# Windowed attention and a two-layer MLP in split fp32: half of the lower weights made on GpSimd, one slice's split queued behind the first activations, four weight loads at another place

## The chip, the cores and the metric

The kernel runs on one core of a Trainium2 chip. A core has TensorE (matmul), VectorE, ScalarE and GpSimd, each with its own queue of instructions, and SyncE, whose queue issues nearly all DMAs here. In the profile they are called PE, DVE, ACT, POOL and SP. The metric is device time in microseconds (us), the median over runs.

## The reference

Batch 8, 8 heads, 512 local and 32 global positions, head size 64; then an MLP of 4352 tokens (8 x 544), width 512, hidden width 2048.

```python
s_g   = scale * q_g @ [k_g, k_l].T               # global queries see all positions
out_g = softmax(s_g) @ [v_g, v_l]
s_ll  = where(|i - j| <= 32, scale * q_l @ k_l.T, -1e9)
s_l   = [scale * q_l @ k_g.T, s_ll]              # local queries see a window and the global keys
out_l = softmax(s_l) @ [v_g, v_l]
x = concat(out_g, out_l), heads side by side     # (4352, 512)
h = x @ w_in                                     # w_in (512, 2048), delivered as float64
out = (h * sigmoid(h)) @ w_out                   # w_out (2048, 512), delivered as float64
```

## The kernel before

**Split numbers.** The MLP's operands are kept as two fp32r numbers, an upper part (the rounded value) and a lower part (the rest); a product is three matmuls: upper by upper, lower by upper, upper by lower. `xh`/`xl` are the parts of x, `gh`/`gl` those of the activations, `w_hi`/`w_lo` those of the weights.

**Weights.** The hidden width is cut into 16 slices f of 128. A slice has two halves of 128x512: half 0 belongs to `w_in` (read by `first_layer`), half 1 to `w_out` (read by `second_layer`). A half goes through three steps. `fetch_weights(f, half)` issues its load, 512 KB of 64-bit words, on SyncE's queue. `join_weights` makes fp32 of it (L221 on ScalarE, L223 and L224 on VectorE). `split_weights(f)` makes both halves' parts: for each half a cast on ScalarE (L233) and a subtraction w - w_hi on VectorE (L234). `raw_w12`, say, is half 0 of slice 6, `raw_w13` half 1 of slice 6. All this is done once, while block 0 runs; the parts then stay in SBUF.

**The MLP.** Tokens come in 12 blocks n of 3 tiles (the last two of 2). For each block, f runs over the 16 slices: `first_layer(n, f)` does 12 matmuls (L625) into `h`, then tanh (L632, ScalarE), one VectorE operation (L633), the cast `gh` (L635, ScalarE) and the rest `gl` (L636, VectorE). `second_layer(n, f-1)` of the slice before follows on TensorE with 9 matmuls (L652), then `first_layer(n, f+1)`, and so on.

**Attention.** It comes in steps k (one chunk of 128 queries, one pair of heads), laid between the MLP's matmuls by `fill`. A step loads q and k (`st_load`, tile `raw`), computes scores (L381 on TensorE), adds the mask (L388, VectorE, from PSUM), takes exp (L392, ScalarE), scales by the reciprocal of the sum (L394, L395 on VectorE; L399, L401 on ScalarE), and is transposed. From step 12 on the transposition goes over DMA: two copies on GpSimd (L413, `halves`), a DMA out (`away`), and a transposing DMA back (`pt`). `st_out` (L464) makes x from it, with `xh` (L471) and `xl` (L472). The global queries have steps of their own (`gs`, `pg`: L266, L269, L292 to L297).

**Order.** TensorE's instructions run in the order in which the program is written. For the other engines a scheduler orders them by its own estimate, save that those wrapped in `hold` keep the program's order among themselves. Each engine works through its queue in order. The steps of attention and the first loads of weights are put on a line of due times (`put(when, ...)`) and sorted. The table `FIRSTW` says which halves are fetched at which step k; `PASSW` says which at slice f of block 0; the remaining ones are fetched five slices ahead (`FETCH`). Slices 0 and 1 are split ahead of block 0. In block 0, at slice f >= 1, `split_weights(f + 1)` and the joins two slices ahead come before `first_layer(0, f)`.

Of the kernel before, what the change touches and what calls it, by code (L numbers as in the profile page):

```python
# [9 lines left out]
F32 = mybir.dt.float32  # L10
# [6 lines left out]
ALU = mybir.AluOpType  # L17
# [12 lines left out]
NCC, NF = DM // P, DFF // P  # L30
# [21 lines left out]
FETCH, LOOK = 5, 3  # L52
PLACES = ("ws15", "ws14", "ws13", "klo", "ws14", "ws15", "klo", "qk")
FIRSTW = {4: ((0, 0), (0, 1)), 5: ((1, 0), (1, 1)), 6: ((2, 0),), 7: ((2, 1),), 8: ((3, 0), (3, 1)),
          9: ((4, 0), (4, 1)), 10: ((5, 0), (5, 1), (7, 0)), 11: ((8, 1), (6, 1))}
PASSW = {0: ((7, 1), (9, 1)), 1: ((10, 1),)}
JOINS, SPLITS = (9.0, 9.6, 10.2, 10.8, 11.4, 12.0), (12.1, 12.7)

FIRST = dict(load=(-1.2, -1.1, -1.0, 0.1), vload=(1.22, 1.23, 2.22, 2.23), turn=(3.2, 4.0, 4.9, 5.8), out=(4.3, 5.2, 6.1, 7.0),
# [9 lines left out]
HEADS0, HEADS = (11, 1), (7, 2)  # L69
TURN1, TURN, TURND = (0.65, 1.5), (0.4, 1.5), (0.4, 0.45)  # L70
FULL = 0.98
END = 0.5

@with_exitstack
def attention_moe_kernel(ctx: ExitStack, tc: tile.TileContext, qk0_in, qk_in, v_in, gqk, wts, out):
    nc = tc.nc
# [27 lines left out]
    hold = tc.keep_in_program_order  # L104
# [83 lines left out]
    w_32, w_hi, w_lo, w_raw, w_next = [], [], [], {}, [0]  # L188
# [18 lines left out]
    def join_weights():  # L207
        i = w_next[0]
        w_next[0] += 1
        f = i // 2  # L210
        if f + 1 == NF:
            w_32.append(work.tile([P, SKV], F32, tag="klo", bufs=BUFS["qk"], name=f"w{i}")[:, :DM])
        elif i % 2 == 0:
            w = const.tile([P, 2 * DM], F32, tag=f"ws{f + 1}", name=f"w{f}")
            w_32.extend((w[:, :DM], w[:, DM:]))
        for raw, c0, n in w_raw[i]:
            join_words(w_32[i][:, c0 : c0 + n], raw)
# [9 lines left out]
    def split_weights(f):  # L227
        w_hi.append(const.tile([P, 2 * DM], F32R, tag=f"wh{f}", name=f"w_hi{f}"))
        w_lo.append(const.tile([P, 2 * DM], F32R, tag=f"ws{f}", name=f"w_lo{f}"))
        for c0 in range(0, 2 * DM, DM):  # L230
            sl = slice(c0, c0 + DM)
            hi, lo, w = w_hi[f][:, sl], w_lo[f][:, sl], w_32[2 * f + c0 // DM]
            hold(nc.scalar.copy(out=hi, in_=w))  # L233
            hold(nc.vector.tensor_tensor(out=lo, in0=w, in1=hi.bitcast(F32), op=ALU.subtract))  # L234


    state = {}
# [279 lines left out]
    at = 0.0  # L517

    def put(when, fn, *a):
        stream.append((when, fn, a))  # L520
# [3 lines left out]
    for k, (t, b, c, pr) in enumerate(steps):  # L524
# [12 lines left out]
        if k == AHEAD:  # L537
# [7 lines left out]
            at = FIRST["then"]  # L545
# [6 lines left out]
                put(at + (TURN1 if b < 2 else TURN if b < GD else TURND)[hh], g_turn, b, hh)  # L552
        for f, half in FIRSTW.get(k, ()):
            put(at + 0.01, fetch_weights, f, half)
        ats.append(at)
        put(min(at + due["load"], ats[k - 3] + BEFORE) if k >= ND + 3 else at + due["load"], st_load, *a)
        put(at + due["split"], st_split, *a)
# [9 lines left out]
        if k < SINGLE or pr == NPR - 1:  # L567
            n = 1 if k < SINGLE else NPR
# [27 lines left out]
    ends, t = [], 0  # L596
    for s in SIZES:
        t += s
        ends.append(marks[t - 1] + END)

# [3 lines left out]
    def fill(part):  # L604
# [4 lines left out]
        if n + 1 < len(SIZES):  # L609
            advance(ends[n] + (ends[n + 1] - ends[n]) * min(1.0, now[1] / total / FULL))  # L610

# [6 lines left out]
    def first_layer(n, f):  # L618
        nt = SIZES[n] * P
        xh, xl = xblk[n]  # L620
        h = ps_h.tile([P, 512], F32, tag="h", name=f"h{n}_{f}")
        i = 0
        for wt, x in ((w_hi[f], xh), (w_hi[f], xl), (w_lo[f], xh)):
            for c in range(NCC):
                nc.tensor.matmul(h[:, :nt], wt[:, c * P : (c + 1) * P], x[:, c, :nt], start=(i == 0),  # L625
                                 stop=(i == 3 * NCC - 1))
                i += 1
        t = two.tile([P, 3 * P], F32, tag="t", bufs=1, name=f"t{n}_{f}")
        gh = two.tile([P, 3 * P], F32R, tag="gh", name=f"gh{n}_{f}")
        gl = two.tile([P, 3 * P], F32R, tag="gl", name=f"gl{n}_{f}")  # L630

        nc.scalar.activation(t[:, :nt], h[:, :nt], AF.Tanh, scale=0.5)  # L632
        nc.vector.scalar_tensor_tensor(out=t[:, :nt], in0=t[:, :nt], scalar=1.0, in1=h[:, :nt], op0=ALU.add,  # L633
                                       op1=ALU.mult)
        nc.scalar.copy(out=gh[:, :nt], in_=t[:, :nt])  # L635
        nc.vector.tensor_tensor(out=gl[:, :nt], in0=t[:, :nt], in1=gh[:, :nt].bitcast(F32), op=ALU.subtract)  # L636
        return gh, gl

    def second_layer(n, f, gh, gl):
# [37 lines left out]
    for n in range(len(SIZES)):  # L677
        for f in range(NF):
            if n == 0:
                split_weights(f + 1) if 0 < f < NF - 1 else None  # L680
                while w_next[0] < 2 * min(NF, f + LOOK):
                    join_weights()
                for g, half in PASSW.get(f, ()):
                    fetch_weights(g, half)
                for g, half in ((f + FETCH, 0), (f + FETCH - (f + FETCH > SCRATCH), 1)):
                    if g < NF and 2 * g + half not in w_raw:
                        fetch_weights(g, half)
            elif f == 0:
                advance(ends[n])
                now[:] = n, 0  # L690
            g = first_layer(n, f)
            fill(SIZES[n])
            if pend is not None:
                second_layer(*pend)
            pend = (n, f, *g)
# [70 lines left out]
```

## Time and profile before

| | |
|---|---|
| median of 3 runs | 965.1 us (964.55 to 967.78) |
| the profiled execution | 964.87 us, span of its profile 962.7 us |
| TensorE busy | 940.6 us (98%) |
| VectorE busy | 629.9 us (65%) |
| ScalarE busy | 574.2 us (60%) |
| GpSimd busy | 217.1 us (23%) |

Times in the profile are counted from the start of the span. Block 0 begins at 47 us and ends at about 142 us; the weights are joined and split from 31 to 133 us. A row of the timeline gives start, duration, engine, line, operation, output <- inputs and their shapes; what stands in brackets is the engine's idle time before it and what ended that.

### The profile page before, as it was taken

What the parts mean: (1) busy time and instruction counts of PE and PEld (TensorE: products, weight loads), DVE (VectorE), ACT (ScalarE), POOL (GpSimd) and SP (SyncE); (2) the same over time, 40 slices, a digit from 0 to 9 for tenths busy, and PEclk for the clock granted to TensorE, in tenths of its full rate; (3) what the DMA queues carried; (4) which work ended last, traced back from release to release, by engine and by line L of the source; (5) the groups of instructions that cost most, each with busy time, mean ns of one, the idle gap of its engine ahead of it and who ended that gap; (6) DMA issues with size and microseconds to landing.
All of it is one profiled execution on the core that took longest, in us unless ns stands there. A gap on an engine that the chain in (4) does not pass through costs nothing.

```text
span 962.7 us, 17396 instructions
## 1 busy us (share of the span) xinstructions
PE 940.6 (98%) x5734; PEld 840.9 (87%) x5734; DVE 629.9 (65%) x1893; ACT 574.2 (60%) x1475; POOL 217.1 (23%) x433
## 2 busy tenths in 40 slices
PE   8789999999999999999999999999999999999998
PEld 6578888999998999989999899998999899989897
DVE  5889977766876677655677677766677656453322
ACT  7888876656656566544665656665566555443322
POOL 2112322122332223122133222222223221120000
PEclk9999999999999999999999999999999999999999
DMA  8989966577668675743856776686775864532000
GB/s 301 350 226 262 266 170 187 158 171 213 172 157 211 168 192 147 193 116 86 223 158 167 201 172 188 159 206 170 170 216 148 201 147 130 144 93 66 1 22 23
DMA packets 201306, 162.57 MB, mean 169 GB/s; under 512 B 139392, under 2 KB 159360, under 8 KB 201216
## 3 DMA queue, kind: packets, MB, share of 16 engines
q1 hardware_dynamic: 196800, 153.52, 59.9%
q10 hardware_dynamic: 4416, 7.93, 2.3%
q8 instruction: 46, 0.75, 0.3%
q14 instruction: 44, 0.36, 0.1%
HBM read 86.44 MB, written 41.94 MB: 133 GB/s over the span
## 4 chain that ended last, share of the span: by engine, by line
PE 83%; DVE 4%; ACT 2%; issue 1%; DMA 0%; DVEq 0%; ACTq 0%
PE h L625 36%; PE out L652 35%; PE o L464 6%; PE s L383 2%; PE s L384 2%; DVE w_lo L234 1%; DVE w L224 1%; PE gs L275 1%; PE gs L276 1%; DVE probs L388 1%; DVE klo L366 0%; DMA raw<-in_qk_dram 0%; DVE raw_w L223 0%; ACT probs L392 0%; DVE t L633 0%
## 5 line engine op out<-in xcount | busy, mean ns | idle before, releaser
L413 POOL COPY halves<-probs 128x512 uint16<-128x512 uint16 x232 | 154.9, 694 | 436.2 <-ACT probs L399 234.6
L632 ACT ACTIVATE t<-h 128x384 f32<-128x384 f32 (+1 forms) x192 | 90.6, 472 | 172.5 <-PE h L625 156.9
L633 DVE SCALAR_TENSOR_TENSOR t<-t,h 128x384 f32<-128x384 f32 (+1 forms) x192 | 101.6, 529 | 105.9 <-ACT t L632 104.8
L652 PE MATMUL out<-w_hi,gh 128*128 128x512 f32 x544 | 164.2, 400 | 2.5 <-ACT gh L635 2.5
L625 PE MATMUL h<-xh,w_hi 128*128 128x384 f32 (+1 forms) x768 | 160.0, 330 | 1.9 <-ACT w_hi L233 1.9
L652 PE MATMUL out<-w_lo,gh 128*128 128x512 f32 x544 | 161.2, 394 | 0.0
L652 PE MATMUL out<-w_hi,gl 128*128 128x512 f32 x544 | 161.0, 394 | 0.0
L625 PE MATMUL h<-xl,w_hi 128*128 128x384 f32 (+1 forms) x768 | 158.2, 327 | 0.0
L625 PE MATMUL h<-xh,w_lo 128*128 128x384 f32 (+1 forms) x768 | 158.2, 327 | 0.0
L392 ACT ACTIVATE probs<-probs,st 128x224 f32<-128x224 f32 x244 | 115.8, 475 | 62.8 <-DVE st L388 62.1
L625 PEld LDWEIGHTS h<-xh,w_hi 128*128 128x128 f32 x768 | 132.9, 188 | 17.4 <-ACT w_hi L233 3.6
L636 DVE TENSOR_TENSOR gl<-t,gh 128x384 fp32r<-128x384 f32 (+1 forms) x192 | 110.3, 575 | 43.1 <-ACT gh L635 40.9
L388 DVE CUSTOM_DVE_ANT_0 probs<-s,mask 128x224 f32<-128x224 f32 x244 | 85.8, 387 | 80.2 <-PE s L384 70.8
L625 PEld LDWEIGHTS h<-xl,w_hi 128*128 128x128 f32 x768 | 132.8, 188 | 0.0
L625 PEld LDWEIGHTS h<-xh,w_lo 128*128 128x128 f32 x768 | 131.3, 188 | 0.5 <-DVE w_lo L234 0.3
L635 ACT CAST gh<-t 128x384 fp32r<-128x384 f32 (+1 forms) x192 | 94.5, 492 | 57.8 <-DVE t L633 57.6
L652 PEld LDWEIGHTS out<-w_hi,gl 128*128 128x128 f32 x544 | 100.3, 188 | 22.2 <-DVE gl L636 0.5
L652 PEld LDWEIGHTS out<-w_lo,gh 128*128 128x128 f32 x544 | 100.5, 188 | 21.7 <-issue 0.6
L652 PEld LDWEIGHTS out<-w_hi,gh 128*128 128x128 f32 x544 | 93.8, 189 | 13.3 <-ACT gh L635 4.7
L365 ACT CAST qk<-raw 128x704 fp32r<-128x704 f32 x100 | 77.5, 775 | 7.7 <-DMA raw<-in_qk_dram 5.2
L366 DVE TENSOR_TENSOR klo<-raw,qk 128x448 fp32r<-128x448 f32 x100 | 66.2, 662 | 18.2 <-ACT qk L365 16.7
L399 ACT ACTIVATE probs<-probs,st 128x224 f32<-128x224 f32 x118 | 56.7, 481 | 30.2 <-DVE st L395 28.7
(96 smaller groups left out, 1065.7 us busy)
## 6 DMA issues: line engine op xcount, KB each, us to landing
raw<-in_qk_dram SPq DMA_DIRECT2D x100, 352.0 KB, 3.2
away<-halves SPq DMA_DIRECT2D x116, 256.0 KB, 2.3
vraw<-in_v_dram SPq DMA_DIRECT2D x30, 512.0 KB, 5.1
raw_w<-in_wts_dram SPq DMA_DIRECT2D x29, 512.0 KB, 6.4
raw_g<-in_gqk_dram SPq DMA_DIRECT2D x32, 304.0 KB, 3.1
out_dram<-o ACTq DMA_DIRECT2D x29, 256.0 KB, 3.3
raw<-in_qk_dram SPq DMA_DIRECT2D x28, 240.0 KB, 4.6
gaway<-pg SPq DMA_DIRECT2D x10, 256.0 KB, 2.1
```

Of the source, the lines that this page charges most:

```text
L365: nc.scalar.copy(out=qk, in_=raw)
L366: nc.vector.tensor_tensor(out=klo[:, :KW], in0=raw[:, QW:], in1=qk[:, QW:].bitcast(F32), op=ALU.subtract)
L388: nc.vector.tensor_tensor_reduce(out=p[:, u, :W], in0=ss[u], in1=mask_of[c], scale=-SCALE, scalar=3.0e38, op0=ALU.add, op1=ALU.min, accum_ ...
L392: nc.scalar.activation(p[:, u, :W], p[:, u, :W], AF.Exp, bias=st[:, u : u + 1], scale=-1.0, accum_out=st[:, 2 + u : 3 + u])
L413: nc.gpsimd.tensor_copy(out=halves[:, :, u], in_=p[:, 2 * P * u : 2 * P * (u + 1)].bitcast(U16).rearrange("p (j h) -> p h j", h=2))
L464: nc.tensor.matmul(o[D * u : D * (u + 1), :m], vraw[:, a, u, :], pt[:, u, a, :m], start=(a == 0), stop=(a == 1))
L625: nc.tensor.matmul(h[:, :nt], wt[:, c * P : (c + 1) * P], x[:, c, :nt], start=(i == 0), stop=(i == 3 * NCC - 1))
L632: nc.scalar.activation(t[:, :nt], h[:, :nt], AF.Tanh, scale=0.5)
L633: nc.vector.scalar_tensor_tensor(out=t[:, :nt], in0=t[:, :nt], scalar=1.0, in1=h[:, :nt], op0=ALU.add, op1=ALU.mult)
L635: nc.scalar.copy(out=gh[:, :nt], in_=t[:, :nt])
L636: nc.vector.tensor_tensor(out=gl[:, :nt], in0=t[:, :nt], in1=gh[:, :nt].bitcast(F32), op=ALU.subtract)
L652: nc.tensor.matmul(outs[n][i], g[:, i * P : (i + 1) * P], w, start=(f == 0 and j == 0), stop=(f == NF - 1 and j == 2))
```

## The change

Three edits:

- In `split_weights`, from slice 2 on the subtraction of the second half (c0 > 0, the `w_out` half) is issued on GpSimd instead of VectorE. That is 14 of 32 subtractions.
- At slice f = 1 of block 0, the instructions of `split_weights(2)` and of the joins of slice 3 are ordered behind the cast `gh` (ScalarE) and the rest `gl` (VectorE) of slice 0, on these two engines.
- The loads (6,1), (7,1), (9,1) and (10,1), that is `raw_w13`, `raw_w15`, `raw_w19` and `raw_w21`, are put at one place, one step after step 12 on the line of due times. Before, (6,1) was fetched at step 11, (7,1) and (9,1) at slice 0 and (10,1) at slice 1 of block 0.

```diff
-          9: ((4, 0), (4, 1)), 10: ((5, 0), (5, 1), (7, 0)), 11: ((8, 1), (6, 1))}
-PASSW = {0: ((7, 1), (9, 1)), 1: ((10, 1),)}
+          9: ((4, 0), (4, 1)), 10: ((5, 0), (5, 1), (7, 0)), 11: ((8, 1),)}
+BEHIND = {12: ((6, 1), (7, 1), (9, 1), (10, 1))}
...
+POOLED = 2
...
             hold(nc.scalar.copy(out=hi, in_=w))
-            hold(nc.vector.tensor_tensor(out=lo, in0=w, in1=hi.bitcast(F32), op=ALU.subtract))
+            engine = nc.gpsimd if f >= POOLED and c0 else nc.vector
+            hold(engine.tensor_tensor(out=lo, in0=w, in1=hi.bitcast(F32), op=ALU.subtract))
...
+        for f, half in BEHIND.get(k, ()):
+            put(at + 1.0, fetch_weights, f, half)
...
-        nc.scalar.copy(out=gh[:, :nt], in_=t[:, :nt])
-        nc.vector.tensor_tensor(out=gl[:, :nt], in0=t[:, :nt], in1=gh[:, :nt].bitcast(F32), op=ALU.subtract)
+        made = (nc.scalar.copy(out=gh[:, :nt], in_=t[:, :nt]),
+                nc.vector.tensor_tensor(out=gl[:, :nt], in0=t[:, :nt], in1=gh[:, :nt].bitcast(F32), op=ALU.subtract))
+        if n == 0 and f == 0:
+            state["made"] = made
...
             if n == 0:
-                split_weights(f + 1) if 0 < f < NF - 1 else None
-                while w_next[0] < 2 * min(NF, f + LOOK):
-                    join_weights()
-                for g, half in PASSW.get(f, ()):
-                    fetch_weights(g, half)
+                with ExitStack() as behind:
+                    for ins in state.pop("made") if f == 1 else ():
+                        behind.enter_context(tc.issue_after(ins.ins))
+                    split_weights(f + 1) if 0 < f < NF - 1 else None
+                    while w_next[0] < 2 * min(NF, f + LOOK):
+                        join_weights()
```

TensorE's queue is the same before and after, instruction by instruction. The other queues differ. In the changed file the lines stand one to four further down: the cast L233 is L234 there, the subtraction L234 is L236, L388 is L390, L632 is L636, L635 is L639. In the names a slice or step comes first and a buffer's number last: `gh0_0_726` is block 0, slice 0.

ScalarE between the last `xh` of block 0 and the cast of `gh` of slice 0, before:

```order
L471 CAST xh_0_242<-o11_685 128x128
L294 ACTIVATE pg0_127,gst1_0_732<-pg0_127,gst1_0_732 128x544
L399 ACTIVATE probs0_85<-probs0_85,st12_651 128x224
L401 ACTIVATE probs0_85<-probs0_85,st12_651 128x224
L233 CAST w_hi2_743<-w2_610 128x512 x2
L221 ACTIVATE w3_749<-raw_w6_477 128x512
L221 ACTIVATE w3_749<-raw_w7_479 128x512
L392 ACTIVATE probs1_86,st13_699<-probs1_86,st13_699 128x224 x2
L632 ACTIVATE t0_0_725<-h0_0_712 128x384
L269 COPY pg1_128<-gs1_2_784 64x272 x2
L635 CAST gh0_0_726<-t0_0_725 128x384
```

and now:

```order
L473 CAST xh_0_242<-o11_683 128x128
L394 ACTIVATE probs1_86,st13_705<-probs1_86,st13_705 128x224 x2
L296 ACTIVATE pg0_127,gst1_0_734<-pg0_127,gst1_0_734 128x544
L401 ACTIVATE probs0_85<-probs0_85,st12_649 128x224
L403 ACTIVATE probs0_85<-probs0_85,st12_649 128x224
L636 ACTIVATE t0_0_727<-h0_0_714 128x384
L401 ACTIVATE probs1_86<-probs1_86,st13_705 128x224
L403 ACTIVATE probs1_86<-probs1_86,st13_705 128x224
L639 CAST gh0_0_728<-t0_0_727 128x384
L234 CAST w_hi2_745<-w2_608 128x512 x2
L222 ACTIVATE w3_751<-raw_w6_477 128x512
L222 ACTIVATE w3_751<-raw_w7_479 128x512
```

The casts of slice 2 and the joins of slice 3 have moved from ahead of the tanh to behind `gh`, and step 13's exp and scaling from behind them to ahead of `gh`.

VectorE at the split of slice 9, the joins of slice 10 and the softmax sums of step 20, before:

```order
L234 TENSOR_TENSOR w_lo9_1254<-w9_1191,w_hi9_1253 128x512 x2
L223 TENSOR_SCALAR raw_w20_1020<-raw_w20_1020 128x512
L224 SCALAR_TENSOR_TENSOR w10_1259<-w10_1259,raw_w20_1020 128x512
L223 TENSOR_SCALAR raw_w21_756<-raw_w21_756 128x512
L394 TENSOR_SCALAR st20_1306<-st20_1306 128x2
L224 SCALAR_TENSOR_TENSOR w10_1259<-w10_1259,raw_w21_756 128x512
L395 RECIPROCAL st20_1306<-st20_1306 128x2
```

and now:

```order
L236 TENSOR_TENSOR w_lo9_1254<-w9_1191,w_hi9_1253 128x512
L224 TENSOR_SCALAR raw_w20_1020<-raw_w20_1020 128x512
L225 SCALAR_TENSOR_TENSOR w10_1259<-w10_1259,raw_w20_1020 128x512
L224 TENSOR_SCALAR raw_w21_698<-raw_w21_698 128x512
L225 SCALAR_TENSOR_TENSOR w10_1259<-w10_1259,raw_w21_698 128x512
L396 TENSOR_SCALAR st20_1306<-st20_1306 128x2
L637 SCALAR_TENSOR_TENSOR t0_9_1353<-t0_9_1353,h0_9_1340 128x384
L397 RECIPROCAL st20_1306<-st20_1306 128x2
```

One of the two subtractions is gone, and the operation behind the tanh of slice 9 has come ahead of the reciprocal. On GpSimd the missing halves stand between the copies of the steps, now:

```order
L236 TENSOR_TENSOR w_lo8_1186<-w8_1089,w_hi8_1185 128x512
L415 COPY halves19_1294<-probs1_86 128x2x256 x2
L236 TENSOR_TENSOR w_lo9_1254<-w9_1191,w_hi9_1253 128x512
L415 COPY halves20_1367<-probs0_85 128x2x256
L236 TENSOR_TENSOR w_lo10_1321<-w10_1259,w_hi10_1320 128x512
```

where before only the copies stood. SyncE's queue around the first `away`, before:

```order
L205 DMA raw_w17_597<-in_wts_dram 128x1024
L205 DMA raw_w13_599<-in_wts_dram 128x1024
L343 DMA raw13_614<-in_qk0_dram 128x480
L241 DMA raw_g1_2_616<-in_gqk_dram 128x608
L343 DMA raw14_673<-in_qk0_dram 128x480
L241 DMA raw_g1_3_675<-in_gqk_dram 128x608
L418 DMA away12_694<-halves12_677 128x1024
L205 DMA raw_w15_708<-in_wts_dram 128x1024
L205 DMA raw_w19_710<-in_wts_dram 128x1024
L343 DMA raw15_739<-in_qk0_dram 128x480
L205 DMA raw_w21_756<-in_wts_dram 128x1024
```

and now:

```order
L206 DMA raw_w17_597<-in_wts_dram 128x1024
L345 DMA raw13_612<-in_qk0_dram 128x480
L243 DMA raw_g1_2_614<-in_gqk_dram 128x608
L345 DMA raw14_671<-in_qk0_dram 128x480
L243 DMA raw_g1_3_673<-in_gqk_dram 128x608
L206 DMA raw_w13_692<-in_wts_dram 128x1024
L206 DMA raw_w15_694<-in_wts_dram 128x1024
L206 DMA raw_w19_696<-in_wts_dram 128x1024
L206 DMA raw_w21_698<-in_wts_dram 128x1024
L420 DMA away12_700<-halves12_675 128x1024
L345 DMA raw15_741<-in_qk0_dram 128x480
```

`raw_w13` has moved behind the loads of steps 13 and 14, the other three from behind `away12` to ahead of it.

## The prediction

> **What bounds the kernel now.** I read the page first (TensorE is busy 98% of the span), then who waited for whom on TensorE, then the busy time by stretches, and last the timelines of the engines around the longest wait. TensorE's own waits between 46 and 140 us, the stretch in which block 0 makes the weights (columns: us in total, times, longest):
>
> ```profile
> PE out L652 <- ACT gh L635: 2.5, 1, 2.5
> PE h L625 <- ACT w_hi L233: 1.9, 3, 1.1
> ```
>
> ```profile
> core 0: us, PE busy (x) PEld busy (x) DVE busy (x) ACT busy (x) POOL busy (x), PEclk, DMA share, GB/s
> 40.00:46.90 6.90, 4.71 (x35) 3.17 (x34) 4.84 (x16) 6.71 (x17) 0.47 (x2) 1.00 0.91 335
> 61.20:97.40 36.20, 35.09 (x200) 30.97 (x199) 33.54 (x94) 32.26 (x82) 8.30 (x15) 1.00 0.89 247
> 97.40:132.30 34.90, 34.05 (x189) 30.09 (x190) 33.00 (x92) 29.73 (x76) 9.74 (x16) 1.00 0.86 239
> 160.00:963.00 803.00, 794.22 (x4835) 717.14 (x4831) 504.42 (x1486) 447.14 (x1137) 180.53 (x342) 1.00 0.58 151
> ```
>
> Three things follow. All that this change touches lies before 140 us. There TensorE has 2.5 us to win in one hole and 1.9 us in three. And from 61 to 132 us VectorE is busy 66.5 of 71.1 us (33.54 + 33.00), more than ScalarE (62.0): it paces the weights. The clock is 1.00 throughout. The chain of waits shows how that pace reaches TensorE at slice 9 (start, us, what):
>
> ```profile
> 95.22 0.50 DVE w L224
> ...
> 95.99 0.48 ACT probs L399
> 96.47 0.37 ACT probs L401
> 96.84 0.52 ACT w_hi L233
> ...
> 97.40 2.35 PE h L625 x12
> ```
>
> VectorE's backlog delays the softmax scaling, this delays the cast of the weights behind it on ScalarE, and `first_layer` waits.
>
> **The long hole.** TensorE, then ScalarE, then the VectorE operations that feed them (start, us, engine, line; in brackets idle time and what ended it):
>
> ```profile
> 46.27 1.02 PE L381 MATMUL s<-raw 128*128 128x224 f32 x4 [1.12 <-DMA raw<-in_qk_dram]
> 51.51 0.68 PE L266 MATMUL gs<-raw_g 128*64 128x272 f32 x4
> 54.70 0.97 PE L652 MATMUL out<-w_hi,gh 128*128 128x512 f32 x3 [2.51 <-ACT gh L635]
> 56.20 0.92 PE L381 MATMUL s<-raw 128*128 128x224 f32 x4
> 57.65 0.87 PE L625 MATMUL h<-xh,w_hi 128*128 128x384 f32 x4
> 59.75 0.86 PE L652 MATMUL out<-w_hi,gh 128*128 128x512 f32 x3
> ```
>
> ```profile
> 47.31 0.27 ACT L471 CAST xh<-o 128x128 fp32r<-128x128 f32 x1
> 48.16 0.75 ACT L294 ACTIVATE pg<-pg,gst 128x544 f32<-128x544 f32 x1 [0.58 <-DVE st L395]
> ...
> 48.90 0.47 ACT L399 ACTIVATE probs<-probs,st 128x224 f32<-128x224 f32 x1
> 49.28 0.47 ACT L401 ACTIVATE probs<-probs,st 128x224 f32<-128x224 f32 x1
> 49.65 1.13 ACT L233 CAST w_hi<-w 128x512 fp32r<-128x512 f32 x2
> 50.68 1.24 ACT L221 ACTIVATE w<-raw_w 128x512 f32<-128x512 f32 x2
> 51.83 0.47 ACT L392 ACTIVATE probs<-probs,st 128x224 f32<-128x224 f32 x1
> ...
> 52.76 0.47 ACT L632 ACTIVATE t<-h 128x384 f32<-128x384 f32 x1
> 53.13 0.76 ACT L269 COPY pg<-gs 64x272 f32<-64x272 f32 x2
> 54.14 0.51 ACT L635 CAST gh<-t 128x384 fp32r<-128x384 f32 x1 [0.25 <-DVE t L633]
> ```
>
> ```profile
> 47.61 0.29 DVE L472 TENSOR_TENSOR xl<-o,xh 128x128 fp32r<-128x128 f32 x1
> 53.55 0.55 DVE L633 SCALAR_TENSOR_TENSOR t<-t,h 128x384 f32<-128x384 f32 x1
> ```
>
> TensorE is done at about 52.1 (51.51 and four matmuls at 0.15) and waits for `gh0_0`; its tanh stood behind slice 2's casts and joins (49.65 to 51.83, 2.18 us) and an exp pair.
>
> **The change, part by part.** *Slice 2's split behind the first activations.* From start to start on ScalarE, L471 takes about 0.15 (0.27 less the overlap of some 0.1 that neighbouring rows show), an exp pair 0.93 (51.83 to 52.76), L294 0.74, L399 with L401 0.75, tanh 0.37. In the new order `gh0_0` is reached at 47.46 + 0.93 + 0.74 + 0.75 + 0.37 + 0.75 = 51.00 and done at 51.5 instead of 54.65. L633, 0.47 on VectorE, fits under the second L399/L401. TensorE then goes on at 52.13 without a hole: 2.57 us won, with 0.6 us in hand. What is late next is `gh0_1`, now queued behind the exp pair of step 14: its scores come at 56.20 - 2.57 = 53.63, their masks 1.07 later (as the rows at 101.67 and 102.74 below stand apart), masks and exps together end at about 56.1, and after L633 the cast at 57.0; TensorE asks at 59.75 - 2.57 = 57.18. It just fits. Slice 2's own casts, now at 51.5 to 52.6, are wanted at 57.65 - 2.57 = 55.08. The casts of slice 3 follow `gh0_1` and one L399/L401 pair at 57.75, where they stood at
>
> ```profile
> 60.62 1.12 ACT L233 CAST w_hi<-w 128x512 fp32r<-128x512 f32 x2
> ```
>
> so the makers of the weights gain 2.9 us there, TensorE 2.6. I take the smaller, **-2.6 us**.
>
> *Four loads.* Of the four, only (6,1) goes later on SyncE's queue; (7,1), (9,1) and (10,1) move from behind the first `away` to ahead of it. (6,1) no longer stands ahead of `raw13`, whose landing ended the wait at 46.27: 512 KB at the 335 GB/s above are 1.6 us. By itself this wins nothing, because `h0_0` needs the xl of 47.61, which hangs on ScalarE, busy for 6.71 of the 6.90 us up to 46.9 and without a gap to 47.5. But the new VectorE order puts step 13's two masks ahead of that xl. With the earlier landing they fit at 46.2 to 46.9; without it xl and the start of `h0_0` come 1.2 us later. The 2 MB now ahead of `away12` take 6.3 us at that rate, from about 41, so `away12` (ready at about 51) and its transpose are little delayed; their reader, `st_out` of steps 12 to 15, comes five slices later. Cost 0; its bad end, 1.2, is rival (c).
>
> *The subtraction on GpSimd.* VectorE loses 14 of 32, each 0.60 us from start to start (the row gives a median 686 ns, of which 0.08 overlaps the next). The nearest prices of GpSimd, and what happens when VectorE runs beside it:
>
> ```profile
> L234 DVE TENSOR_TENSOR w_lo<-w,w_hi x32: 673/686/1100, 42.9 to 132.3; 128x512 fp32r<-128x512 f32 x32
> L413 POOL COPY halves<-probs x232: 604/614/1152, 49.4 to 875.9; 128x512 uint16<-128x512 uint16 x116
> 41.80 0.24 POOL L440 COPY pt<-pgt 128x64 f32<-128x64 f32 x1 [3.41 <-PE o L464]
> 73.22 1.38 POOL L413 COPY halves<-probs 128x512 uint16<-128x512 uint16 x2 [8.17 <-ACT probs L399]
> 73.29 0.84 DVE L223 TENSOR_SCALAR raw_w<-raw_w 128x512 uint32<-128x512 uint32 x1
> 75.11 0.42 DVE L223 TENSOR_SCALAR raw_w<-raw_w 128x512 uint32<-128x512 uint32 x1
> 101.67 0.92 PE L381 MATMUL s<-raw 128*128 128x224 f32 x4
> 102.59 1.17 POOL L413 COPY halves<-probs 128x512 uint16<-128x512 uint16 x2 [4.04 <-DMA away<-halves]
> 102.74 0.39 DVE L388 CUSTOM_DVE_ANT_0 probs<-s,mask 128x224 f32<-128x224 f32 x1 [0.92 <-PE s L381]
> ```
>
> No row shows GpSimd subtracting. Its copy costs 0.24 us for 64 elements and 0.61 for 512, so 0.43 us go to the elements. That is just what L223 loses beside it (0.84 against 0.42): VectorE, reading SBUF alone, stands still while GpSimd streams. L388, which reads PSUM, loses nothing. A subtraction reads twice as many elements: estimate 0.86 us of hold in an operation of 1.04. Bounds: not under the copy's hold, 0.43; not over its longest row less the fixed 0.18, 0.97. I take 0.86. VectorE's loss to one: in the new order L223 follows the half that VectorE keeps, then, in 7 of slices 4 to 15, a join that could start only 0.15 later anyway, since ScalarE's L221 follows the two casts: 0.71 lost. In the other five a pair of masks from PSUM (0.39 each, overlapping, some 0.6) or other such work runs under it: 0.25. Against 0.60 saved each: 7 x 0.11 - 5 x 0.35 = **-1.0 us** on the pacing engine, within the 1.9 us of waits for w_hi. If VectorE lost only what the present copies cost it, a quarter of the hold (0.2), 12 x 0.4 = 4.8 would be saved, of which TensorE can use those 1.9 and some 0.9 of slow starts behind its holes: -2.8. If 0.97 were lost every time: +4.4. The second half is not needed before `second_layer` of its slice, which comes 2.10 + 2.95 + 2.10 = 7.1 us after `first_layer` of that slice begins (57.65 to 59.75, 54.70 to 57.65, and again); GpSimd's lateness, a pair of copies (1.17) and a subtraction, 2.2 us, is covered by that. What queues behind it on GpSimd are the copies of later steps and, through SyncE, their loads; in the new order each stands behind a subtraction whose cast ScalarE reaches before that step's scaling, so it adds at most 1.04 us to a path with microseconds to spare.
>
> **Sum.** 964.87 (the profiled execution; the median, 965.1, stands 0.2 higher) - 2.6 + 0 - 1.0 = **961.3**. After 140 us TensorE bounds nearly all and its order is the same, so the gain should be kept.
>
> **The rule that speaks against it.** The Trainium skill, "SBUF — State Buffer", section "Who interferes with whom", says that GpSimd and a VectorE operation with two SBUF inputs or in a two-port mode exclude each other for the whole instruction. The rows at 73 us agree in kind, but show 0.43 of 0.61 us. This is rival (a) below. By the whole 1.04 the last bound would be 12 x 0.44 = +5.3 in place of +4.4. The skill's "GPSIMD Engine Reference", section "3.1 Elementwise — side-by-side cycle accounting", gives 4497 ns for 2048 elements, an estimate of 1.12 us here; with that held each time the sum would be 968.5.
>
> **Rivals.** (a) *The lock decides, and it ends slower.* GpSimd's subtraction becomes ready just as VectorE ends its half, so it goes first and holds VectorE's next joins in full in every slice. At 0.86 that is 12 x 0.26 = +3.1: 965.4; at 0.97 966.7. From 0.60 + 2.6/12 = 0.82 us lost per slice the kernel is slower than before. For: at 73 us VectorE lost the whole stream. Against: in five slices PSUM work comes next. (b) *The lock hardly counts*, as with the present copies: 964.87 - 2.6 - 2.8 = 959.5. For: the median of the 32 subtractions stays at 686 ns, though copies run among them. Against: their maximum is 1100, and the new operation is longer and comes just ahead of the joins. (c) *The hole closes in part*: `raw13` doesn't land earlier, xl is 1.2 us late: 962.5. (d) *Nothing is kept*: block 1 waits for loads that don't come sooner, 964.9. For: 803.0 less 794.2 leaves 8.8 us after 160 us that this change doesn't fill. Against: the loads there follow buffers that TensorE frees, so they move with it.
>
> **Chances.** Forecast 0.45, (a) 0.20, (b) 0.18, (c) 0.10, (d) 0.07. A run can tell 0.3%, 2.9 us. Faster by more: (b) and three quarters of the forecast, 0.52. Slower by more needs (a) above its own bound, with other mishaps: 0.12. The rest 0.36. Range 959.2 to 966.9: (b) less a little, (a) at its upper price; the forecast's own is 960 to 962.5.
>
> **What would show it.** Right: `out` of slice 0 starts near 52.1 with no hole over 0.5; GpSimd's subtraction near 1.04 us; VectorE's L223/L224 lengthened by up to 0.9 right behind its half, L388 not; the cast of slice 3 near 57.8, slice 15's near 126 (130 now); `raw13`'s wait gone. Wrong: TensorE's waits for w_hi grow past 4 us, GpSimd takes over 1.3, or block 1 begins where it did.

## The result, and the profile after

The changed kernel takes 975.87 us (median of 5 runs, 974.55 to 977.21) against 965.1 before; the ratio is 1.010, 95% interval 1.0085 to 1.0116. It is slower by 10.8 us, where 961.3 was forecast. The profiled execution took 974.55 us, with a span of 972.4.

The page's row of busy time after, then the end of block 0 in both kernels (after, then before). "151.0 to 152.4" are the starts of the first and the last of the three copies that take block 0's results out of PSUM:

```profile
PE 943.6 (97%) x5734; PEld 841.5 (87%) x5734; DVE 639.4 (66%) x1879; ACT 573.4 (59%) x1475; POOL 238.7 (25%) x447
```

```profile
L670 ACT ACTIVATE o<-out x3: 600/602/602, 151.0 to 152.4; 128x512 f32<-128x512 f32 x3
```

```profile
L664 ACT ACTIVATE o<-out x3: 600/601/602, 140.6 to 142.0; 128x512 f32<-128x512 f32 x3
```

Block 0 ends 10.4 us later; the rest of the span is 821.4 us against 822.1. So all of the loss lies before 151 us. VectorE has 14 instructions fewer and is busy 9.5 us longer (639.4 against 629.9).

The first edit did at its place what was forecast. TensorE around slice 0 in the kernel after:

```profile
48.73 0.85 PE L629 MATMUL h<-xh,w_hi 128*128 128x384 f32 x4
50.91 0.68 PE L268 MATMUL gs<-raw_g 128*64 128x272 f32 x4
51.52 0.97 PE L658 MATMUL out<-w_hi,gh 128*128 128x512 f32 x3
57.79 0.97 PE L658 MATMUL out<-w_hi,gh 128*128 128x512 f32 x3 [1.06 <-ACT gh L639]
```

`second_layer` of slice 0 begins at 51.52 without a hole (54.70 before, behind 2.51 us of waiting). Then TensorE's three longest waits from 46 to 150 us and the busy time of two stretches, after (the columns as in the prediction):

```profile
PE h L629 <- ACT w_hi L234: 6.9, 5, 2.1
PE out L658 <- ACT gh L639: 2.4, 4, 1.1
PE o L466 <- ACT pgt L329: 1.5, 1, 1.5
```

```profile
61.20:97.40 36.20, 32.23 (x182) 27.81 (x181) 32.43 (x75) 27.38 (x68) 16.60 (x19) 1.00 0.71 194
97.40:132.30 34.90, 29.83 (x164) 24.78 (x162) 31.07 (x78) 24.66 (x64) 13.74 (x17) 1.00 0.84 235
```

The waits for `w_hi` have grown from 1.9 to 6.9 us, the sign that the prediction named as "wrong". In the same 71.1 us TensorE does 62.1 us of work instead of 69.1. And VectorE gets through 153 instructions (75 + 78) where it got through 186 (94 + 92), though it is busy nearly as long: each takes longer. What lengthens them is seen in GpSimd's group of the 14 subtractions and in the timelines of GpSimd and VectorE around two of them, slice 2's and slice 8's, with VectorE at the subtraction of slice 12 in the last row:

```profile
L236 POOL TENSOR_TENSOR w_lo<-w,w_hi 128x512 fp32r<-128x512 f32 x14 | 19.4, 1387 | 26.9 <-ACT w_hi L234 20.9 <-issue 5.0 <-POOL pt L442 0.5
...
52.15 1.30 POOL L236 TENSOR_TENSOR w_lo<-w,w_hi 128x512 fp32r<-128x512 f32 x1 [1.66 <-ACT w_hi L234]
53.39 1.84 POOL L415 COPY halves<-probs 128x512 uint16<-128x512 uint16 x2
94.88 1.50 POOL L236 TENSOR_TENSOR w_lo<-w,w_hi 128x512 fp32r<-128x512 f32 x1 [0.19 <-ACT w_hi L234]
```

```profile
52.19 1.55 DVE L224 TENSOR_SCALAR raw_w<-raw_w 128x512 uint32<-128x512 uint32 x1
53.84 0.90 DVE L225 SCALAR_TENSOR_TENSOR w<-w,raw_w 128x512 uint32<-128x512 uint32 x1
54.67 0.83 DVE L224 TENSOR_SCALAR raw_w<-raw_w 128x512 uint32<-128x512 uint32 x1
95.15 1.52 DVE L224 TENSOR_SCALAR raw_w<-raw_w 128x512 uint32<-128x512 uint32 x1
...
121.32 0.42 DVE L224 TENSOR_SCALAR raw_w<-raw_w 128x512 uint32<-128x512 uint32 x1
```

GpSimd needs 1.27 us at the least and 1.39 in the mean. The join that VectorE runs beside it takes 1.52 or 1.55 us instead of 0.42: 1.1 us lost, against 0.60 saved. In slices 4, 5 and 15 it is VectorE's own subtraction that is held (1.73 to 1.79 us instead of 0.69). Behind the subtraction GpSimd's queued copies follow at once (53.39) and lengthen the next joins too (0.90 and 0.83 instead of 0.69 and 0.42). Of the fourteen, only slice 12's cost next to nothing (121.32: VectorE was already at its join when GpSimd began at 121.6, and PSUM work came next). The thirteen VectorE operations beside the others are 0.92 to 1.13 us longer than usual, 14.1 in all.

How much VectorE was held in all, the copies behind included, can be counted: 14 subtractions of 0.69 us are gone, 9.7 us of busy time. Against the kernel `e1_vector` below, which differs in these alone and is busy 633.5 us, that leaves 639.4 - (633.5 - 9.7) = 15.6 us of holding, 1.11 for each subtraction. Such a count is rough: two kernels with the same VectorE instructions, the one before and `e1_vector`, differ by 3.6 us themselves (629.9 and 633.5), that is 0.26 for each subtraction. From start to start a VectorE subtraction is 0.60, so VectorE's path got 14 x (1.11 - 0.60) = 7.1 us longer.

### The profile page after: what moved, and what is told of

It reads as the page before. It is cut to its first block, busy times and chain, and to the rows that moved or that the text cites. A ratio compares the mean times of both kernels' runs of the same rounds, so it can differ in the third digit from the quotient of the medians.

```text
span 972.4 us, 17417 instructions
## 1 busy us (share of the span) xinstructions
PE 943.6 (97%) x5734; PEld 841.5 (87%) x5734; DVE 639.4 (66%) x1879; ACT 573.4 (59%) x1475; POOL 238.7 (25%) x447
## 4 chain that ended last, share of the span: by engine, by line
PE 82%; DVE 4%; ACT 2%; issue 1%; DVEq 0%; ACTq 0%
PE h L629 35%; PE out L658 35%; PE o L466 6%; PE s L385 2%; PE s L386 2%; DVE w L225 1%; ACT probs L394 1%; PE gs L277 1%; PE gs L278 1%; DVE raw_w L224 1%; DVE klo L368 1%; ACT qk L367 0%; ACT probs L401 0%; DVE qk L369 0%; DVE probs L390 0%
## 5 line engine op out<-in xcount | busy, mean ns | idle before, releaser
L415 POOL COPY halves<-probs 128x512 uint16<-128x512 uint16 x232 | 157.3, 705 | 399.0 <-ACT probs L401 213.9
L636 ACT ACTIVATE t<-h 128x384 f32<-128x384 f32 (+1 forms) x192 | 90.6, 472 | 175.0 <-PE h L629 157.3
L390 DVE CUSTOM_DVE_ANT_0 probs<-s,mask 128x224 f32<-128x224 f32 x244 | 86.0, 387 | 79.8 <-PE s L386 70.2
L639 ACT CAST gh<-t 128x384 fp32r<-128x384 f32 (+1 forms) x192 | 94.6, 493 | 64.3 <-DVE t L637 64.1
```

The source lines that it names most:

```text
L390: nc.vector.tensor_tensor_reduce(out=p[:, u, :W], in0=ss[u], in1=mask_of[c], scale=-SCALE, scalar=3.0e38, op0=ALU.add, op1=ALU.min, accum_ ...
L415: nc.gpsimd.tensor_copy(out=halves[:, :, u], in_=p[:, 2 * P * u : 2 * P * (u + 1)].bitcast(U16).rearrange("p (j h) -> p h j", h=2))
L639: made = (nc.scalar.copy(out=gh[:, :nt], in_=t[:, :nt]), nc.vector.tensor_tensor(out=gl[:, :nt], in0=t[:, :nt], in1=gh[:, :nt].bitcast(F32 ...
```

## The experiments

A comparison within the traces needs a common start, because block 0 begins up to 3 us earlier or later from run to run. I take the time from the first matmul of `first_layer(0, 1)` (48.73 after; 49.34 before) to the first copy of block 0's result: 91.3 us before, 102.3 after. "Block 0" below means this time. Each experiment was timed beside runs of the kernel before, whose median was then 966.1 to 966.3 us; the ratios are to these. Names of lines move with the edits.

### The edits one by one

`e1_vector`: the changed kernel, all subtractions on VectorE.

```diff
-POOLED = 2
+POOLED = 16
```

> The changed kernel with every lower weight subtracted on VectorE again; the other two edits stay. Theory T (the subtractions on GpSimd hold VectorE still, about 1.1 us each, and that is the whole loss): the long hole stays closed, TensorE's waits for w_hi go back to about 2 us, block 0 ends 2.6 to 3.2 us earlier than in the kernel before, 961.5 to 962.7 us. Rival S (the new order of the queues, from the split behind the first activations and from the loads, costs the time, and GpSimd only a little): 970 us or more, with waits for w_hi over 4 us.

Measured 966.8 us beside 966.25 for the kernel before, ratio 1.0004 (0.9996 to 1.0013); block 0 92.5 us, waits for `w_hi` 3.7. Both theories miss. The subtractions on GpSimd cost nearly everything (102.3 against 92.5), but the 2.6 us of the closed hole, which T expected to see, aren't there either, though the hole is closed.

`e2_pool_alone`: the kernel before, only the subtraction moved.

```diff
+            engine = nc.gpsimd if f >= 2 and c0 else nc.vector
-            hold(nc.vector.tensor_tensor(out=lo, in0=w, in1=hi.bitcast(F32), op=ALU.subtract))
+            hold(engine.tensor_tensor(out=lo, in0=w, in1=hi.bitcast(F32), op=ALU.subtract))
```

> The kernel before with nothing but the 14 subtractions on GpSimd. T: the long hole stays (2.5 us) and the holes in front of slices 3 to 15 come on top; what the changed kernel lost after its first gain, 13 us, is lost here too: 976 to 979 us, slower than the changed kernel. S: 963 to 967 us. If part of the loss needs the other edits (slices closer to each other leave less room), it lies between, 970 to 975 us.

Measured 983.47 us, ratio 1.0177 (1.0164 to 1.0191); block 0 109.3 us. The sign is T's, the size more than it expected. With slice 2 still split ahead of the first activations, GpSimd's first subtraction lengthens the very hole that was to close, from 2.51 to 4.10 us; and a second hole, of 3.89 us, opens at 90.75, where TensorE waits for a copy (`pgt`) that stands behind late casts and joins of the weights on ScalarE. VectorE's first held join, then TensorE at the two holes:

```profile
51.12 1.50 DVE L223 TENSOR_SCALAR raw_w<-raw_w 128x512 uint32<-128x512 uint32 x1
```

```profile
55.96 1.52 PE L653 MATMUL out<-w_hi,gh 128*128 128x512 f32 x3 [4.10 <-ACT gh L636]
90.75 2.40 PE L465 MATMUL o<-pt,vraw 128*64 128x160 f32 x16 [3.89 <-ACT pgt L328]
```

`e3_behind_alone`: the kernel before, only the split and joins behind the first activations (the `issue_after` block of the diff, loads and subtraction as before).

> The kernel before with nothing but slice 2's split and slice 3's joins behind the first activations. T, with the forecast's reading of the loads (they matter only in that raw13 lands in time): the hole in front of out of slice 0 closes, and the start of h0_0 comes up to 1.2 us later, since the masks of step 13 wait for raw13 ahead of xl: 962.3 to 963.8 us. If the loads don't matter at all: the same as the kernel with both edits, 961.5 to 962.7 us. S: slower than before.

Measured 967.33 us, ratio 1.0015 (1.0005 to 1.0024); block 0 93.2 us. All three expectations miss but S's sign: the hole is down to 0.39 us and yet nothing is won.

`e4_loads_alone`: the kernel before, only the four loads moved (`BEHIND` as in the diff, `PASSW` empty).

> The kernel before with nothing but the four loads at their new place. The wait of TensorE for raw13 (1.12 us at 46.3) is gone or short, h0_0 starts as before since it hangs on ScalarE, and all else is as before: 964.5 to 965.5 us, the same. If away12 is late behind the 2 MB of weights: a wait in front of the sums of slices 5 to 6, up to 2 us slower.

Measured 966.1 us, ratio 1.0001 (0.9992 to 1.0009): by themselves the loads cost and win nothing, as the prediction had it. What they are worth together with the split is the step from `e3_behind_alone` to `e1_vector`, 1.0015 against 1.0004, and these intervals overlap.

### Where the closed hole's gain went

In `e1_vector` the order of VectorE and ScalarE is another one than before, not only at the edit but up to the end of block 0, since the scheduler places all of it anew. VectorE, then ScalarE, in `e1_vector` at the split of slice 8 (the last row is later, at 119.97):

```profile
85.58 0.69 DVE L225 SCALAR_TENSOR_TENSOR w<-w,raw_w 128x512 uint32<-128x512 uint32 x1
86.19 0.42 DVE L224 TENSOR_SCALAR raw_w<-raw_w 128x512 uint32<-128x512 uint32 x1
86.53 0.42 DVE L474 TENSOR_TENSOR xl<-o,xh 128x256 fp32r<-128x256 f32 x1
86.99 0.38 DVE L390 CUSTOM_DVE_ANT_0 probs<-s,mask 128x224 f32<-128x224 f32 x1
```

```profile
82.41 1.12 ACT L234 CAST w_hi<-w 128x512 fp32r<-128x512 f32 x2
87.41 0.48 ACT L394 ACTIVATE probs<-probs,st 128x224 f32<-128x224 f32 x1 [1.83 <-DVE st L390]
90.98 1.13 ACT L234 CAST w_hi<-w 128x512 fp32r<-128x512 f32 x2
...
119.97 0.52 ACT L639 CAST gh<-t 128x384 fp32r<-128x384 f32 x1 [1.58 <-DVE t L637]
```

and in the kernel before the first of those masks, and ScalarE at the same two casts:

```profile
86.00 0.38 DVE L388 CUSTOM_DVE_ANT_0 probs<-s,mask 128x224 f32<-128x224 f32 x1
```

```profile
83.49 1.13 ACT L233 CAST w_hi<-w 128x512 fp32r<-128x512 f32 x2
90.16 1.12 ACT L233 CAST w_hi<-w 128x512 fp32r<-128x512 f32 x2
```

The masks now stand behind two more operations of the joins and an `xl`; ScalarE waits 1.83 us for them and reaches the next cast 8.57 us after the last one, where it took 6.67. So 1.9 us are lost in one slice (the next cast, 5.96 us later against 6.59, brings 0.6 back), and at 119.97 ScalarE waits 1.58 for an operation that VectorE has put behind three operations of joins.

`e5_old_order`: `e1_vector`, with VectorE's and ScalarE's rows from slice 3's subtraction (slice 2's `gh` on ScalarE) to the end of block 0 tied in the order of the kernel before.

```diff
+    for engine, row, n in ((mybir.EngineType.DVE, DVE_ORDER, 1636), (mybir.EngineType.Activation, ACT_ORDER, 1202)):
+        mine = [i for i in nc.cur_bb.bb.instructions if i.engine == engine and type(i).__name__ not in LEFT]
+        for a, b in zip(row, row[1:]):
+            tc.add_manual_dep(mine[b], mine[a].name, mybir.DependencyInfo(mybir.DependencyClass.NoSync, mybir.DependencyReason.DATA))
```

> The changed kernel with every lower weight subtracted on VectorE, and with VectorE's and ScalarE's instructions from the subtraction of slice 3 to the end of block 0 fixed in the order of the kernel before (ordering edges without waits). The hole stays closed. Theory O (what the hole gave was lost again to the new order of these two engines in slices 4 to 15): waits for w_hi back to about 2 us, slice 15's casts near 127.5, 962 to 963.5 us, ratio 0.996 to 0.998. Rival P (the makers of the weights set the end whatever the order; a hole closed early only moves the wait): waits for w_hi of 3.5 us or more, 965.5 to 967 us, ratio 1.000.

Measured 964.27 us, ratio 0.9983 (0.9974 to 0.9993), waits for `w_hi` 2.1 us, block 0 90.0 us. Time and ratio lie a little above O's range, and P's 1.000 is outside the interval. Against `e1_vector`, from which it differs in the order alone, block 0 is 2.5 us shorter: the new order took the gain back. Against the kernel before, 1.3 of the 2.6 us are kept (91.3 to 90.0); where the other 1.3 went is not shown.

### What GpSimd's subtraction costs, and by what

`e6_pool_old_order`: `e5_old_order` with the 14 subtractions on GpSimd (`POOLED = 2`), the order tied in the same way.

> The kernel of e5_old_order with the 14 subtractions on GpSimd; VectorE's and ScalarE's order is the same but for the 14 that are gone. Theory T (GpSimd's subtraction holds VectorE, about 1.1 us against 0.6 saved, and shifts GpSimd's copies onto the joins): 9 to 11 us above e5_old_order, 971 to 975 us. Rival O2 (the scheduler's order in the changed kernel is what makes the subtraction dear): under 5 us above e5_old_order.

Measured 970.7 us, ratio 1.0044 (1.0032 to 1.0056); 6.4 us above `e5_old_order`, block 0 96.7 against 90.0. It lies between the two expectations: the subtraction is dear in either order, but the new order adds some 3 us to its price (102.3 - 92.5 = 9.8 there, 6.7 here). In the old order masks or an `xl` stand beside more of the subtractions. VectorE's busy time, of `e6_pool_old_order` and then of `e5_old_order`:

```profile
PE 943.8 (97%) x5734; PEld 841.2 (87%) x5734; DVE 635.6 (66%) x1879; ACT 573.8 (59%) x1475; POOL 240.3 (25%) x447
```

```profile
PE 942.2 (98%) x5734; PEld 841.6 (87%) x5734; DVE 631.5 (66%) x1893; ACT 573.7 (60%) x1475; POOL 217.3 (23%) x433
```

By the count used above, VectorE was held 635.6 - (631.5 - 9.7) = 13.8 us, 0.98 each; its path became 14 x 0.38 = 5.3 us longer.

`e7_memset`: the changed kernel, with zeros written in place of the subtraction.

```diff
+            if engine is nc.gpsimd:
+                hold(nc.gpsimd.memset(lo.bitcast(F32), 0.0))
```

> The changed kernel with GpSimd writing zeros over those 14 halves in place of the subtraction: an operation at the same place, with the same wait for the cast, that reads nothing, estimated at half a microsecond. The lower parts of 14 of the w_out halves are left out of the result. VectorE's and ScalarE's order is that of the changed kernel up to the end of block 0. T: VectorE's joins beside it are lengthened by no more than its length; 14 x 0.6 are saved and at most 14 x 0.5 lost: 962 to 967 us. Rival O (the order of the changed kernel costs the 10 us by itself): 972 us or more.

Measured 963.94 us, ratio 0.9979 (0.9969 to 0.9988), block 0 89.9 us: in the changed kernel's own order of VectorE, with another operation of GpSimd in place of the subtraction, all of the loss is gone. But a memset is also shorter (0.64 us in the mean), and it runs earlier. The expectation has it wait for the cast; it doesn't, since it reads nothing: it begins up to 8.1 us before its cast ends, where the subtractions begin 0.08 to 0.15 us behind theirs. `e9_memset_twice` takes the first away: two of them, one behind the other, the order tied to the changed kernel's.

```diff
+                for _ in range(2):
+                    hold(nc.gpsimd.memset(lo.bitcast(F32), 0.0))
```

> The kernel of e7_memset with every memset done twice, one right behind the other, so that GpSimd is busy about as long (2 x 0.64 us) as with the subtraction (1.39); the order of VectorE, ScalarE and GpSimd in block 0 is that of the changed kernel. The lower parts of 14 of the w_out halves are left out of the result. Theory T (the price is what GpSimd takes from VectorE: 1.1 us for a subtraction, 0.3 for a memset): 0.6 lost against 0.6 saved, 962 to 966 us. Rival L (the price is that GpSimd is late: its copies, and the loads behind them, wait for it): 970 us or more.

The group of the memsets, four of them with the join that VectorE runs beside them, and the page's row of busy time:

```profile
L258 POOL MEMSET w_lo<- 128x512 f32 x28 | 17.4, 624 | 4.0 <-ACT w L242 3.2
```

```profile
124.00 2.49 POOL L258 MEMSET w_lo<- 128x512 f32 x4
124.53 0.42 DVE L244 TENSOR_SCALAR raw_w<-raw_w 128x512 uint32<-128x512 uint32 x1
125.05 0.69 DVE L245 SCALAR_TENSOR_TENSOR w<-w,raw_w 128x512 uint32<-128x512 uint32 x1
```

```profile
PE 941.2 (98%) x5734; PEld 841.2 (87%) x5734; DVE 626.6 (65%) x1879; ACT 573.1 (60%) x1475; POOL 233.2 (24%) x461
```

Measured 964.83 us, ratio 0.998 (0.9969 to 0.9992), block 0 89.8 us. GpSimd is busy with them for 17.4 us, nearly the 19.4 of the subtractions, at the same places of its queue, and the kernel is no slower. So it is not GpSimd's longer work that costs. Its lateness (L) is tested in part only: GpSimd sat idle 4.0 us ahead of these memsets and 26.9 ahead of the subtractions, which wait for their casts, so the copies behind them could start earlier too. `e11_vector_longer` below bears on the rest.

What differs is VectorE: 626.6 us busy instead of 639.4, in the same order. Beside a memset the two operations of a join keep their usual 0.42 and 0.69 us (124.53 and 125.05 above), where beside a subtraction they took 1.52 (95.15) and, in slice 6 of the changed kernel, 1.61. The Trainium skill, "SBUF — State Buffer", section "Who interferes with whom", says that a VectorE instruction with two SBUF inputs contends with a GpSimd instruction that reads SBUF, not with one that only writes it. The trace agrees for L245, which has two inputs; of L244, which has one and is the operation held most often, that sentence doesn't speak. Counted as for the changed kernel, two memsets hold VectorE 626.6 - 623.8 = 2.8 us over 14, or 0.2 each, no more than the roughness of such a count.

`e11_vector_longer`: the opposite test. GpSimd does nothing new, VectorE is made longer.

```diff
+            if f >= 2 and c0:
+                part = lo[:, :304]
+                hold(nc.vector.tensor_tensor(out=part, in0=part.bitcast(F32), in1=part.bitcast(F32), op=ALU.max))
```

> The kernel of e5_old_order (no GpSimd subtraction) with VectorE made longer by hand: right behind each of the 14 subtractions stands one more VectorE operation, a maximum of 304 columns of the result with itself, estimated at 0.39 us from start to start, 5.5 us in all. That is what GpSimd's subtraction cost VectorE in e6_pool_old_order beyond what it saved (VectorE's busy time 635.6 against 631.5, with 14 x 0.69 us of work gone: 0.98 us held each, 0.38 net). T: the same end as e6_pool_old_order, 969 to 971.5 us. If GpSimd's lateness had a large part in e6_pool_old_order: 966 to 968 us.

VectorE's group of the added operation, and TensorE's waits from 46 to 150 us in this kernel:

```profile
L258 DVE TENSOR_TENSOR w_lo<-w_lo 128x304 fp32r<-128x304 f32 x14 | 7.7, 548 | 0.5
```

```profile
PE h L651 <- ACT w_hi L253: 5.0, 7, 1.9
PE out L680 <- ACT gh L661: 1.6, 3, 0.8
```

Measured 969.45 us, ratio 1.0028 (1.0016 to 1.004), block 0 96.3 us. As T had it. The 14 operations take 7.7 us, less 0.08 of overlap each 6.6, and block 0 is 6.3 us longer than in `e5_old_order`: what is added to VectorE's path there arrives at the end nearly one for one, and by the same waits (4.2 and 1.3 us in `e6_pool_old_order`). Of the 6.7 us that block 0 lost in `e6_pool_old_order`, the 5.3 on VectorE's path thus give some 5.1. The rest, 1.6, is about what a stretch at half TensorE clock cost there, at 99.9 us (last section); `e11_vector_longer` has none. That leaves little for GpSimd's lateness.

`e8_pieces`: the subtraction in four pieces, order as in the changed kernel.

```diff
+            n = DM // 4 if engine is nc.gpsimd else DM
+            for q in range(0, DM, n):
+                hold(engine.tensor_tensor(out=lo[:, q : q + n], in0=w[:, q : q + n], in1=hi[:, q : q + n].bitcast(F32), op=ALU.subtract))
```

> The changed kernel with each GpSimd subtraction in four pieces of 128 columns, VectorE's and ScalarE's order fixed as in the changed kernel. If GpSimd keeps VectorE off for one whole instruction at a time, VectorE's next operation waits for one piece, estimated 0.4 us, and not for 1.1, and slips in between: 968 to 973 us. If the two simply share a fixed amount of access to SBUF, the sum of the holds stays: 975 to 980 us.

Measured 976.37 us, ratio 1.0108 (1.0092 to 1.0123), as the changed kernel, which would speak for the second reading. The trace says otherwise. GpSimd's four pieces, VectorE beside them, and TensorE after block 0:

```profile
98.22 3.07 POOL L258 TENSOR_TENSOR w_lo<-w,w_hi 128x128 fp32r<-128x128 f32 x4 [3.54 <-ACT w_hi L254]
```

```profile
98.74 0.76 DVE L245 SCALAR_TENSOR_TENSOR w<-w,raw_w 128x512 uint32<-128x512 uint32 x1
99.42 0.68 DVE L244 TENSOR_SCALAR raw_w<-raw_w 128x512 uint32<-128x512 uint32 x1
100.21 0.77 DVE L245 SCALAR_TENSOR_TENSOR w<-w,raw_w 128x512 uint32<-128x512 uint32 x1
```

```profile
160.25 0.34 PE L408 MATMUL s<-qk 128*128 128x224 f32 x1 [3.83 <-DVE qk L392]
```

VectorE slips in between the pieces and loses 0.08, 0.26 and 0.08 us; block 0 takes 97.4 us, 4.9 less than with whole subtractions. What is won there is lost at 160 us, where TensorE waits 3.83 for a step whose load landed late, and runs at half clock behind it. That GpSimd, busy 3.07 us for what took 1.4, delayed the copies and with them SyncE's queue is the likely reason; no run tested it.

`e10_seven`: the changed kernel with `POOLED = 9`, half of the subtractions.

> The changed kernel with the subtraction on GpSimd from slice 9 on only, 7 of the 14. T with a price for each one: half of the 9.4 us between the changed kernel and e1_vector, 970 to 972 us. If the first ones are free, because VectorE has some slack left before it sets the pace: 966 to 969 us.

Measured 968.21 us, ratio 1.002 (1.0008 to 1.0032), block 0 94.9 us, 2.4 above `e1_vector`. The first seven cost more than the last seven, so it is not a fixed price for each; the order here is a third one, so how much of this is slack stays open.

`e12_four`: `e5_old_order` with the subtraction on GpSimd in four slices, chosen because VectorE reads PSUM next.

```diff
-POOLED = 2
+POOLED = (4, 5, 8, 11)
...
-            engine = nc.gpsimd if f >= POOLED and c0 else nc.vector
+            engine = nc.gpsimd if f in POOLED and c0 else nc.vector
```

> The kernel of e5_old_order with the subtraction on GpSimd in slices 4, 5, 8 and 11 only, where VectorE's next work in that order reads PSUM (masks, xl) for some 0.6 us. T: what is left of the hold, some 0.6 us, is about what is saved: 963.5 to 965 us, as e5_old_order. If PSUM work gives no cover, four times the mean price of e6_pool_old_order (6.4 us over 14): 966 to 967 us.

GpSimd and VectorE in slice 8 of this kernel:

```profile
89.79 1.50 POOL L255 TENSOR_TENSOR w_lo<-w,w_hi 128x512 fp32r<-128x512 f32 x1 [0.20 <-ACT w_hi L253]
```

```profile
89.21 0.92 DVE L255 TENSOR_TENSOR w_lo<-w,w_hi 128x512 fp32r<-128x512 f32 x1 [1.04 <-ACT w_hi L253]
90.05 0.38 DVE L409 CUSTOM_DVE_ANT_0 probs<-s,mask 128x224 f32<-128x224 f32 x1
90.67 0.90 DVE L243 TENSOR_SCALAR raw_w<-raw_w 128x512 uint32<-128x512 uint32 x1
```

Measured 963.67 us, ratio 0.9973 (0.9961 to 0.9986), block 0 89.7 us. The masks run at their usual 0.38 while GpSimd subtracts, and the join behind them loses 0.48 instead of 1.1 (the 0.92 of VectorE's subtraction ahead of them is there in the kernel before too, at 90.80). In the other three slices the joins lose 0.43, 0.48 and 0.05. With the cover the subtraction is not seen to cost anything. This version beats both kernels, by 2.4 us the one before; against `e5_old_order` the intervals overlap.

## Why the prediction was wrong, step by step

Two terms of the sum failed. The subtraction on GpSimd was put at -1.0 us and made VectorE's path some 7 us longer instead; and the 2.6 us of the closed hole, put down as kept, were lost again in the slices behind it.

**The long hole: right at its place, wrong in what stays.** `out` of slice 0 began 3.18 us earlier, 0.61 of it because block 0 itself began earlier: 2.57, the forecast to the digit. The cast of slice 3 came at 58.40 (57.75 forecast), and `gh0_1`, "it just fits", was 1.06 us late. The step that failed is the sentence that the makers of the weights gain 2.9 us there and TensorE 2.6, read as a gain for good. It took the pace of slices 4 to 15 as unchanged, while the scheduler gave these slices a new order, and that order lost 1.9 us in slice 8 alone. `e1_vector` (nothing kept) and `e5_old_order` (1.3 us kept) show it: the order is worth 2.5 us of block 0. What took the other 1.3 us of the gain is open. This is rival (d)'s outcome with another mechanism.

**Four loads: right.** `e4_loads_alone` measured 1.0001, and the wait for `raw13` is gone in the changed kernel.

**The subtraction on GpSimd: the mis-sized term.** Forecast -1.0 us; measured +9.8 in block 0 in the new order, +6.7 in the old one. Three of its numbers were off, all one way. The operation takes 1.27 us or more, not 1.04: the price was built from the copies' time for each element, and a subtraction is slower than twice that. (The two copies compared moved 64 fp32 and 512 uint16 elements, as their rows show; no run tells how much of the error is the type.) The hold was 1.1 us, not 0.86; the upper bound of 0.97 came from the copy's longest row, and a row of another operation bounds nothing above. And five slices were to be covered by PSUM work; in the run one was. GpSimd mostly begins about 0.55 us after the start of VectorE's half, and so meets the join that stands right behind it. With the measured 1.11 in all fourteen (the prediction counted the twelve of slices 4 to 15) the prediction's own sum is 14 x 0.51 = +7.1, and `e11_vector_longer` shows that VectorE's path passes this on nearly whole. With nothing kept of the hole that gives 972, and with the 1.5 us of slower matmuls of the last section 973.5; about 1 us up to the 974.55 of the profiled execution stays open.

**Rival (a) was the mechanism**, "goes first and holds VectorE's next joins in full in every slice"; its upper price, 966.7, was too low for the same reason. The figure of the Trainium skill's "GPSIMD Engine Reference", section "3.1 Elementwise — side-by-side cycle accounting", from which 1.12 us and 968.5 were estimated, came nearer than the rows: as the time held, 1.12 is about the 1.11 counted; as the length of the operation it is short of the 1.27 measured at the least.

**GpSimd's lateness: right, as far as is shown.** It was costed at nothing. `e11_vector_longer` comes to within 1.3 us of `e6_pool_old_order` (969.45 and 970.7) without any subtraction on GpSimd, and `e9_memset_twice` shows that longer work on GpSimd alone costs nothing.

## What to carry to other kernels

Moving an operation off a pacing engine helps only if the new engine doesn't hold the old one: compare what is held with what is saved, and test it from both sides, with an operation of the same length that reads nothing, and by making the pacing engine longer by the same amount. Where the hold can't be avoided, place the operation beside work that reads PSUM. And where a scheduler orders the queues, an edit in one place moves the rest: a gain there is kept only if the order behind it is looked at, or tied.

## What the runs showed of the hardware beside this

TensorE's granted clock fell to half for 3.4 us (6.8 in one case) behind holes. First the kernel before around its hole of 2.51 us, then the changed kernel in two stretches (the last column but two is the clock), and its matmuls there:

```profile
52.88:56.29 3.41, 1.59 (x7) 1.32 (x8) 2.37 (x8) 2.86 (x7) 0.81 (x2) 1.00 0.89 281
```

```profile
130.66:134.07 3.41, 1.44 (x6) 0.53 (x4) 2.41 (x12) 2.62 (x8) 0.60 (x2) 1.00 0.31 64
134.07:137.49 3.42, 3.21 (x10) 3.21 (x11) 3.06 (x4) 3.12 (x9) 2.01 (x3) 0.50 0.46 149
```

```profile
134.28 1.65 PE L629 MATMUL h<-xh,w_hi 128*128 128x384 f32 x4 [2.07 <-ACT w_hi L234]
135.72 1.48 PE L629 MATMUL h<-xl,w_hi 128*128 128x384 f32 x4
```

Four matmuls took 1.48 us instead of 0.86, in all about 1.5 us lost. The same came behind the holes of 4.10, 3.89 and 2.08 us in `e2_pool_alone`, 1.95 in `e6_pool_old_order`, 2.00 and 3.83 in `e8_pieces`, and once ahead of block 0 in `e10_seven`, but not behind the 2.51 in the kernel before. The Trainium skill, "TensorE: Matmul & The Clock Gate", "Part 1: The HAM clock gate (the "warmup" mystery)", tells of half rate after an idle window of about 3.4 us that runs freely. The length of the slow stretch agrees; that holes of about 2 us sufficed does not follow from a whole idle window.

The traces tell what counted. In `e2_pool_alone` the clock changes at 56.13, 59.55, 90.26, 97.09, 141.46 and 144.88 us, each a whole number of 3.413 us after the one before: the windows lie on a fixed grid. In these traces, ahead of the kernels' last few us, the clock fell eight times, and in the window of the grid ahead of each fall TensorE was busy 0.01 to 1.47 of the 3.41 us. In every other window at full clock up to there it was busy 1.59 us or more. So it is not the length of a hole but TensorE's busy share in a window: the 2.51 us in the kernel before (from 52.19) lay across the border of two windows, at 52.88, and left 1.59. An estimate from 1.47 and 1.59: the bound lies between 43% and 47%.
